# Sixteen K loads, one of them split into three DMAs: 64 partitions over 16 steps, and twice 32 partitions over 8 steps

## The chip, the cores and the metric

The kernel runs on one core of one Trainium2 chip. Its time is the device time of one execution in microseconds (us). An execution is also profiled; the profile's times are counted from the first instruction of the span.

## What is computed

One decode step (one new token, batch 8, width 512): attention over the last 2048 positions of a key/value cache with 32 query heads on 8 key/value heads, and then a small MLP block. For a sequence of one token the shifted branch of the MLP block is zero. Cut to what matters:

```python
W = 2048                                   # the last W of 8192 positions
q = layernorm(x) @ wq                      # (8, 32 heads, 128)
k, v = k_cache[:, :, Sk-W:, :], v_cache[:, :, Sk-W:, :]   # (8, 8, 2048, 128) bf16 each
p = softmax(q @ k^T * 128**-0.5)           # 4 query heads share one k and v
h = x + (p @ v) @ wo                       # wo (4096, 512)
x1 = layernorm(h)                          # the shifted branch adds 0
out = h + x1 + gelu(layernorm(x1) @ w3) @ w4
```

All inputs are bf16. The K and V windows are 33.5 MB each, 79 MB are read in all.

## The kernel before

The 64 pairs of batch and key/value head are called items, i = 8 * batch + head. One loop over steps `p` puts out the program for all engines; each engine works its instructions off in that order and waits on semaphores. At step p the loop emits:

- for p a multiple of 4, one K load (`load_k`, L337) for the four items p to p+3. There are 16 such loads, j = p // 4. Load j goes to buffer j % 3 of `knat` and has that buffer's semaphore;
- the 16 TensorE transposes of item p (`pe_T`, L244, recorded on L249), in two halves, and their copies from PSUM to `kT_sb` (`evict`, L256), one half by ScalarE (L257) and one by VectorE (L259);
- at p = 15, 23, 31 and 39 one of four loads of `wo`;
- the scores of item p - 2 (`pe_QK`, L263, recorded on L269) and, once a batch is complete, the steps of its softmax;
- the V load of item p - 13 (`load_v`, L343, 13 buffers) and its product with the probabilities (L327).

Loads of w3 and of w4 in three parts follow. All these loads but the small one of x are issued by SyncE, one after another in this order, on one queue (q1; recorded on L176). SyncE waits before a load until its buffer is free, and everything behind it waits too. The load of x (`x_sb`, 8 rows of 1 KB) is issued by ScalarE on its own queue (q10).

A K load moves 2 MB. A cache window of one item is 2048 rows of 128 elements. It is read as 32 runs of 64 rows, 16 KB each, and the run a of the item t goes to partition 4a + t, so that each of the 128 partitions gets one run:

```python
dma(SP, knat[:, j % NK, :],
    A_k_cache[i // G, i % G:i % G + KQ, W0:SK, :].rearrange("t (a c) d -> a t (c d)", c=KQ * NC),
    sem_k[j % NK], e_Thi.get(i + KQ - 1 - KQ * NK))
```

The last line is the load's semaphore and its wait: the transposes of the load that used the buffer before. A transpose of item i waits until `sem_k` of its buffer has 16 for every load into it so far (`K`, L236).

After the last item the tail runs: the last products, `wo`, the sums for the layernorm, `uT` (L460), the products with w3 (L475), the gelu (L500), the products with w4 (L513, which waits for the gelu and for the parts of w4) and the output.

Of the kernel before, what the change touches and what calls it, by code (L numbers as in the profile page):

```python
# [15 lines left out]
G = 8  # L16
R = H // G
SK = 8192
W = 2048
W0 = SK - W  # L20
NC = W // 128
# [5 lines left out]
NK = 3  # L27
KQ = 4
# [3 lines left out]
LV = 13  # L32
WO_AT = (15, 23, 31, 39)
NR = 4


class Engine:
# [29 lines left out]
def bass_sequential_preLN__sliding_block_cached__mixer_s_mlp__decode_kernel(  # L67
# [23 lines left out]
    with es:  # L91
# [28 lines left out]
        knat = sb([128, NK, KQ * NC * DH], dt.bfloat16, "knat")  # L120
# [46 lines left out]
        sem_k = [S(f"sem_k{i}") for i in range(NK)]  # L167
# [4 lines left out]
        PE, AC, DV, PO, SP = (Engine(S(n)) for n in ("s_pe", "s_act", "s_dve", "s_pool", "s_sp"))  # L172

        def dma(eng, dst, src, sem, *waits):
            def f(e):
                e.dma_start(dst, src).then_inc(sem, 16)  # L176
            eng.op(f, *waits, inc=False)
# [55 lines left out]
        e_Tlo, e_Thi, e_lo, e_hi, e_QK, e_PV = {}, {}, {}, {}, {}, {}  # L233
        e_max, e_mT, e_neg, e_negps, e_negc, e_exp, e_PT, e_pT, e_lsel, e_Lb, e_rL, e_scale = ({} for _ in range(12))

        def K(i):  # L236
            return sem_k[i // KQ % NK], 16 * (i // KQ // NK + 1)

        def V(i):
            return sem_v[i % NV], 16 * (i // NV + 1)  # L240
# [3 lines left out]
        def pe_T(i):  # L244
            def half(lo):
                def f(e):
                    for n in range(lo, lo + NC // 2):
                        r = NC * (n % KQ) + NC // KQ * (i % KQ) + n // KQ
                        ins = e.matmul(kT_ps[i % 2][:, n * 128:(n + 1) * 128],  # L249
                                       knat[:, i // KQ % NK, r * DH:(r + 1) * DH], ident_b[:, :], is_transpose=True)  # L250
                    return ins
                return f
            e_Tlo[i] = PE.op(half(0), K(i), e_lo.get(i - 2), e_idb)
            e_Thi[i] = PE.op(half(NC // 2), e_hi.get(i - 2))
# [79 lines left out]
                         e_rL[b], e_oz, *waits)  # L334


        def load_k(i):  # L337
            j = i // KQ
            dma(SP, knat[:, j % NK, :],
                A_k_cache[i // G, i % G:i % G + KQ, W0:SK, :].rearrange("t (a c) d -> a t (c d)", c=KQ * NC),  # L340
                sem_k[j % NK], e_Thi.get(i + KQ - 1 - KQ * NK))

        def load_v(i):  # L343
            dma(SP, vnat[:, i % NV, :].rearrange("p (c d) -> p c d", c=NC),
# [9 lines left out]
        def pe_wo_row(g):  # L354
            def f(e):
                for r in range(R):
                    h = R * g + r
                    ins = e.matmul(hrow[32 * r:32 * (r + 1), :], oT_all[:, h, :], wo_v[:, h, :],  # L358
                                   start=(g == 0), stop=(g == NR - 1),
                                   tile_position=(0, 32 * r), skip_group_check=True)  # L360
                return ins
            e = PE.op(f, e_sc7[g], e_scale[NB - 2], (sem_wo, 16 * len(WO_AT)))
            if g == NR - 1:

                e = AC.op(lambda e: e.activation(hr[:, 0, :], hrow, ACT.Copy), e)  # L365
                e_wo.append(DV.op(lambda e: e.tensor_tensor(hr[:, 1, :], hrow, hr[:, 0, :], ALU.subtract), e))


        def pe_h0():
            def f(e):  # L370
                for nb in range(KC):
                    e.matmul(hT_ps[:, nb * B:(nb + 1) * B], x_sb[:, nb * 128:(nb + 1) * 128],
                             ident_b[0:B, 0:B], start=(nb == 0), stop=False, skip_group_check=True)
                for part in range(2):
                    for nb in range(KC):
                        ins = e.matmul(hT_ps[:, nb * B:(nb + 1) * B], hr[:, part, nb * 128:(nb + 1) * 128], selb[:, :],
                                       start=False, stop=False, skip_group_check=True)
                return ins
            PE.op(f, e_wo[-1], e_exp[NB - 2], X, e_selb)

        def pe_wo(g):
            def f(e):
                for h in range(R * g, R * (g + 1)):
                    for nb in range(KC):
                        ins = e.matmul(hT_ps[:, nb * B:(nb + 1) * B], wo_v[:, h, nb * 128:(nb + 1) * 128],
                                       oT_all[:, h, 0:B], start=False, stop=(h == H - 1), skip_group_check=True)
                return ins
            e_wo.append(PE.op(f, e_sc7[g]))
# [3 lines left out]
        for p in range(NITEM + LV + 1):  # L392
            if p < NITEM:
                if p % KQ == 0:
                    load_k(p)
                pe_T(p)
                evict(p)
            if p in WO_AT:
                n = WO_AT.index(p)
# [18 lines left out]
            i = p - LV  # L418
            if 0 <= i < NITEM:
# [7 lines left out]
                else:  # L427
                    dst = kbank[g % 3][:, 0:R]
# [3 lines left out]
            g = i - 1 - G * LAST  # L432
            if g == NR:
                pe_h0()
            if 0 <= g < NR:
                pe_wo_row(g)
            elif g >= NR:
                pe_wo(g)
# [5 lines left out]
        for n in range(3):  # L444
            lo, hi = W4_AT[n:n + 2]
# [117 lines left out]
```

## Time and profile before

| | |
|---|---|
| Time, median of 3 runs (lowest to highest) | 200.28 us (200.23 to 200.66) |
| Time of the profiled execution | 200.67 us |
| Its span in the profile | 198.6 us |
| TensorE busy | 158.0 us (80%) |
| ScalarE busy | 84.7 us (43%) |
| VectorE busy | 70.6 us (36%) |
| Moved by DMA | 79.56 MB, 401 GB/s over the span |
| K loads: 16 of 2048 KB, median from issue to landing | 19.1 us |
| V loads: 64 of 512 KB, median from issue to landing | 19.6 us |
| Mean granted TensorE clock | 0.882 |

A busy engine is not yet the one that bounds the time: the chain of waits, followed back from the last instruction, tells what the end hung on. A DMA's time to landing runs from its issue to its completion and contains the time that it stands in the queue behind other loads. The DMA share is the mean over the core's 16 DMA engines, so a share of half can be eight engines at work and eight idle. A load is cut into packets, one for each contiguous run, and each engine that takes part ends with one small completion packet.

### The profile page before, as it was taken

How to read it: one execution, taken by the hardware profiler on the slowest of the kernel's cores; microseconds unless marked ns; L12 is line 12 of the kernel's file. 1: busy time of each engine (PE TensorE's matmuls, PEld its weight loads, DVE VectorE, ACT ScalarE, POOL GpSimd, SP SyncE). 2: the span in 40 equal slices, each digit the busy share in tenths (PEclk: the TensorE clock that was granted, in tenths of full speed). 3: DMA queues.
4: the chain of work that ended last, by engine and by line, in shares of the span. 5: the costliest groups of instructions: out<-in, count | busy, mean ns of one | idle time of the engine just before them, and what ended most of it. 6: DMA issues, size and time to landing. Idle time of an engine off the chain costs nothing.

```text
span 198.6 us, 5886 instructions
## 1 busy us (share of the span) xinstructions
PE 158.0 (80%) x2725; PEld 117.5 (59%) x2725; DVE 70.6 (36%) x167; ACT 84.7 (43%) x92; POOL 3.5 (2%) x11
## 2 busy tenths in 40 slices
PE   0037999889999299947999199969997999969853
PEld 0037766567766277635776076747774767556753
DVE  6101545533543033511444024422542344233240
ACT  6001666864574037522465045544554464420330
POOL 7000000000000000000000000000000000000000
PEclk9999999999999669995799969996999699965555
DMA  6999999999999999999999999999999999999970
GB/s 233 449 412 429 426 422 398 422 407 434 412 396 436 406 452 392 414 422 420 429 394 437 406 439 409 449 398 450 395 443 405 443 403 416 419 417 416 404 244 23
DMA packets 18280, 79.56 MB, mean 401 GB/s; under 512 B 1480, under 2 KB 7376, under 8 KB 16080
## 3 DMA queue, kind: packets, MB, share of 16 engines
q1 hardware_dynamic: 18240, 79.18, 97.3%
q8 instruction: 21, 0.34, 0.6%
q14 instruction: 3, 0.02, 0.0%
q10 hardware_dynamic: 16, 0.01, 0.0%
HBM read 79.18 MB, written 0.01 MB: 399 GB/s over the span
## 4 chain that ended last, share of the span: by engine, by line
DMA 66%; PE 28%; SPq 4%; issue 0%; DVE 0%
DMA knat<-in_A_k_cache_dram 56%; PE kT_ps L249 16%; DMA w_sb<-in_B_w_dram 10%; PE S_ps L269 6%; SPq L176 4%; PE oT_ps L327 3%; PE S_ps L513 1%; PE sm L305 0%; PE sm L282 0%; PE sm L317 0%; PE sm L291 0%; PE sm L521 0%; DVE fT L518 0%; DVE out_sb L522 0%
## 5 line engine op out<-in xcount | busy, mean ns | idle before, releaser
L257 ACT ACTIVATE kT_sb<-kT_ps 128x1024 bf16<-128x1024 bf16 x64 | 65.6, 1024 | 89.8 <-PE kT_ps L249 89.8
L249 PE MATMUL kT_ps<-ident_b,knat 128*128 128x128 bf16 x1024 | 76.0, 234 | 18.3 <-DMA knat<-in_A_k_cache_dram 18.3
L249 PEld LDWEIGHTS kT_ps<-ident_b,knat 128*128 128x128 bf16 x1024 | 65.5, 106 | 24.2 <-DMA knat<-in_A_k_cache_dram 19.2
L259 DVE COPY kT_sb<-kT_ps 128x1024 bf16<-128x1024 bf16 x64 | 44.3, 692 | 93.2 <-PE kT_ps L249 93.2
L327 PEld LDWEIGHTS oT_ps<-pT_sb,vnat 128*128 128x128 bf16 x896 | 26.5, 97 | 24.6 <-issue 22.3
L269 PE MATMUL S_ps<-kT_sb,qblk 128*32 128x512 bf16 x256 | 41.1, 611 | 0.0
L327 PE MATMUL oT_ps<-pT_sb,vnat 128*128 128x4 bf16 x896 | 31.3, 165 | 0.0
L295 ACT ACTIVATE P_sb<-S_ps,negcol 128x512 bf16<-128x512 f32 x8 | 11.2, 1401 | 5.9 <-DVE negcol L294 5.9
L269 PEld LDWEIGHTS S_ps<-kT_sb,qblk 128*32 128x32 bf16 x256 | 7.2, 94 | 5.4 <-issue 1.4
L219 PE MATMUL S_ps<-xlnT,wbig 128*128 128x8 bf16 x128 | 3.6, 168 | 7.7 <-DMA wbig<-in_A_wq_dram 7.7
L219 PEld LDWEIGHTS S_ps<-xlnT,wbig 128*128 128x128 bf16 x128 | 3.5, 104 | 7.8 <-issue 7.8
L278 DVE TENSOR_REDUCE mcol<-S_ps 128x1 f32<-128x512 f32 x8 | 5.5, 682 | 1.9 <-PE S_ps L269 1.9
L305 PE MATMUL sm<-ident_b,P_sb 128*128 128x128 bf16 x32 | 3.3, 231 | 2.7 <-ACT P_sb L295 2.7
L327 PEld LDWEIGHTS kT_ps<-pT_sb,vnat 128*128 128x128 bf16 x128 | 4.2, 106 | 1.8 <-issue 1.3
L226 DVE TENSOR_SCALAR qblk<-S_ps 128x32 bf16<-128x32 f32 x8 | 0.9, 182 | 11.1 <-PE S_ps L219 11.1
L309 DVE COPY pT_sb<-sm 128x512 bf16<-128x512 bf16 x8 | 3.3, 417 | 3.4 <-PE sm L305 3.4
L327 PE MATMUL kT_ps<-pT_sb,vnat 128*128 128x4 bf16 x128 | 4.5, 167 | 0.0
L207 PE MATMUL sm<-ident_b,xln_b 8*128 8x8 bf16 x4 | 0.3, 175 | 5.2 <-DVE xln_b L198 5.2
L305 PEld LDWEIGHTS sm<-ident_b,P_sb 128*128 128x128 bf16 x32 | 2.1, 102 | 3.2 <-ACT P_sb L295 3.2
L365 ACT ACTIVATE hr<-kT_ps 128x512 bf16<-128x512 f32 x1 | 0.6, 597 | 6.6 <-PE kT_ps L358 6.6
L317 PE MATMUL sm<-lsel,ones_f 128*128 128x32 f32 x16 | 3.2, 281 | 0.3 <-DVE lsel L313 0.3
L291 PE MATMUL sm<-ones_f,negrow 1*128 1x1 f32 x16 | 3.2, 266 | 0.1
(75 smaller groups left out, 63.2 us busy)
## 6 DMA issues: line engine op xcount, KB each, us to landing
knat<-in_A_k_cache_dram SPq DMA_DIRECT2D x16, 2048.0 KB, 19.1
vnat<-in_A_v_cache_dram SPq DMA_DIRECT2D x64, 512.0 KB, 19.6
wbig<-in_A_wq_dram SPq DMA_DIRECT2D x1, 4096.0 KB, 12.3
wbig<-in_A_wo_dram SPq DMA_DIRECT2D x4, 1024.0 KB, 21.6
w_sb<-in_B_w_dram SPq DMA_DIRECT2D x1, 1792.0 KB, 17.9
w_sb<-in_B_w_dram SPq DMA_DIRECT2D x1, 1280.0 KB, 20.1
w_sb<-in_B_w_dram SPq DMA_DIRECT2D x1, 384.0 KB, 17.5
w_sb<-in_B_w_dram SPq DMA_DIRECT2D x1, 128.0 KB, 7.6
```

The costliest lines, as they stand in the source:

```text
L176: e.dma_start(dst, src).then_inc(sem, 16)
L219: ins = e.matmul(S_ps[0][:, h * B:(h + 1) * B], wq_v[:, kc, h * DH:(h + 1) * DH], xlnT[:, kc * B:(kc + 1) * B], start=(kc == 0), stop=(kc ...
L249: ins = e.matmul(kT_ps[i % 2][:, n * 128:(n + 1) * 128], knat[:, i // KQ % NK, r * DH:(r + 1) * DH], ident_b[:, :], is_transpose=True)
L257: e_lo[i] = AC.op(lambda e: e.activation(kT_sb[:, i % NKT, 0:W // 2], kT_ps[i % 2][:, 0:W // 2], ACT.Copy), e_Tlo[i], e_QK.get(i - NKT))
L259: e_hi[i] = DV.op(lambda e: e.tensor_copy(kT_sb[:, i % NKT, W // 2:W], kT_ps[i % 2][:, W // 2:W]), e_Thi[i], e_QK.get(i - NKT))
L269: ins = e.matmul(S_ps[b % 2][32 * u:32 * (u + 1), :], qblk[:, b, g - g % KQ + t, :], kT_sb[:, i % NKT, :].rearrange("p (n t) -> p t n", t= ...
L278: e_max[b] = DV.op(lambda e: e.tensor_reduce(mcol[:, :], S_ps[b % 2][:, :], AX.X, ALU.max), e_QK[G * b + G - 1], e_mT.get(b - 1))
L291: e_negps[b] = PE.op(lambda e: e.matmul(sm[:, NEG], negrow[0:1, :], ones_f[0:1, 0:1], start=True, stop=True), e_neg[b], e_ones)
L295: e_exp[b] = AC.op(lambda e: e.activation(P_sb[:, j, :].rearrange("p (c a w) -> p c w a", c=4, w=KQ), S_ps[j][:, :].rearrange("p (c w a) - ...
L305: ins = e.matmul(pT_ps[:, jt * 128:(jt + 1) * 128], P_sb[:, j, 128 * jt:128 * (jt + 1)], ident_b[:, :], is_transpose=True)
L309: e_pT[b] = DV.op(lambda e: e.tensor_copy(pT_sb[:, j, :, :].rearrange("p (q jt) h -> p q jt h", jt=4), pT_ps[:, 0:NC * H].rearrange("p (jt ...
L327: ins = e.matmul(dst, vnat[:, i % NV, c * DH:(c + 1) * DH], pT_sb[:, b % 2, (c + NC // KQ * (i % KQ)) % NC, R * g:R * (g + 1)], start=(c = ...
```

## The change

The load j = 8 (items 32 to 35, the K of batch 4's first four heads) is issued as three DMAs. The first takes the runs 0 to 15 and writes partitions 0 to 63; the second and the third take 8 runs each and write partitions 64 to 95 and 96 to 127. The same bytes go to the same places. The three share the buffer's semaphore, so the load adds 48 to it in place of 16, and the transposes that wait for this buffer (j = 8, 11 and 14) wait for 32 more. All other loads stay as they are, and the instructions of TensorE, VectorE, ScalarE and GpSimd keep their order.

```diff
+K8 = 8
...
         def K(i):
-            return sem_k[i // KQ % NK], 16 * (i // KQ // NK + 1)
+            j = i // KQ
+            return sem_k[j % NK], 16 * (j // NK + 1 + (2 if j >= K8 and j % NK == K8 % NK else 0))
...
         def load_k(i):
             j = i // KQ
-            dma(SP, knat[:, j % NK, :],
-                A_k_cache[i // G, i % G:i % G + KQ, W0:SK, :].rearrange("t (a c) d -> a t (c d)", c=KQ * NC),
-                sem_k[j % NK], e_Thi.get(i + KQ - 1 - KQ * NK))
+            src = A_k_cache[i // G, i % G:i % G + KQ, W0:SK, :].rearrange("t (a c) d -> a t (c d)", c=KQ * NC)
+            dst = knat[:, j % NK, :]
+            if j == K8:
+                for lo, n in ((0, 16), (16, 8), (24, 8)):
+                    dma(SP, dst[KQ * lo:KQ * (lo + n), :], src[lo:lo + n], sem_k[j % NK],
+                        e_Thi.get(i + KQ - 1 - KQ * NK))
+            else:
+                dma(SP, dst, src, sem_k[j % NK], e_Thi.get(i + KQ - 1 - KQ * NK))
```

## The prediction

> **What bounds the kernel now.** I read the page's chain and DMA queues first, then the chain in order of time near the end, the DMA's busy share by slices over the last 10 us, and SyncE's timeline around the changed load.
>
> ```profile
> DMA 66%; PE 28%; SPq 4%; issue 0%; DVE 0%
> q1 hardware_dynamic: 18240, 79.18, 97.3%
> q8 instruction: 21, 0.34, 0.6%
> q10 hardware_dynamic: 16, 0.01, 0.0%
> ```
>
> The chain is two thirds DMA, and q1, SyncE's queue, keeps the 16 engines at work for 97.3% of the span. The kernel is a stream of loads that hardly pauses. A load has landed when the slowest engine has done its share, so the slowest engine sets the pace.
>
> ```profile
> 142.68 21.14 DMA knat<-in_A_k_cache_dram
> 163.82 0.05 issue
> 163.87 1.07 PE kT_ps L249 x16
> ...
> 174.12 20.07 DMA w_sb<-in_B_w_dram
> 194.19 0.14 issue
> 194.33 1.65 PE S_ps L513 x56
> ```
>
> In the chain (start, length, what) the last K load lands at 163.82 and the big w4 part at 194.19. TensorE had idled only 0.47 us before 163.87: it follows the K landings closely. From there the compute path reaches the end of the last gelu (L500) at 193.75 + 0.39 = 194.14. Loads and compute arrive at L513 together.
>
> ```profile
> DMA  9999999999999999998655555554622222110000
> ```
>
> This is the DMA share from 186 to 196 us in slices of 0.25 us. It falls to half and stays there from 191.0 to 192.75, then to a fifth and to nothing. Half of the engines have nothing left while the other half works on for 2 us and more. The packet records of the trace say who they are. Packets of one engine follow each other at exact distances (16 KB 0.607 us, 4 KB 0.155 us), so the 16 sequences can be told apart. Eight of them also carry q8's 21 code fetches of 16 KB in turn, and each fetch holds its engine up by 1.42 us. Call these the heavy engines and the others the light ones. The heavy ones end each load later:
> - V18, the load just before the changed one: light mean 83.63, heavy mean 85.10, lag 1.47 us
> - the changed load, K8: light up to 89.10, heavy up to 90.70
> - the last K load: light up to 160.81, heavy up to 163.82
> - the last V load: light up to 182.03, heavy up to 186.08
>
> **The change part by part.** *Packets.* Before, K8 gave each engine 8 packets of 16 KB. The first part has 64 packets over 16 steps, four for each of 16 engines. The other two have 8 steps of 4 each. How a load of 8 steps spreads is shown by q10: x_sb has 8 rows, and its 16 packets are 8 of data and 8 completions, so eight engines. (q1's sum confirms the counting: 144 for wq, 80 x 144 for K and V, 4 x 1040 for wo, 528 + 1840 for w3 and w4, and 48 for the output make 18240, with 16 completions each.) So the two small parts go to eight engines, four packets each time. These eight now have 12 packets, the rest 4: +4 x 0.607 = +2.43 us and -2.43 us.
>
> *Which eight.* Three of x_sb's engines can be followed by their exact distances, and as far as the sequences can be told apart all three are light ones. I take it that the eight are the light engines. The Trainium skill ("DMA: Bandwidth & Descriptors", on why a DMA increments its semaphore by 16) says it is the lowest-numbered ones on this path; the trace has no engine numbers, so no row confirms that.
>
> *Best case, every engine at its own rate.* Light engines end K8 at 89.10 + 2.43 = 91.53 instead of 90.70 overall (+0.8). The last K lands at max(160.81 + 2.44, 163.82 - 2.43) = 163.25 (-0.57), the last V at 184.47 (-1.6), and w3 and w4 behind it likewise.
>
> *Worst case, two engines that write the same partitions halve each other.* Every load but the small x_sb spreads over 128 partitions, and the packet distances stay rigid however far the engines drift apart. That is what one sees if every engine has its own eight partitions and meets nobody there. The change is the first to break this: partitions 0 to 63 are written by all 16 engines, then 64 to 127 by eight, while the heavy engines, which must own half of the 128, write them too. Pair a light engine with the heavy one whose partitions it enters, lag d. In the first part the light one is alone for d and shares the remaining 2.43 - d, which takes twice as long. While the heavy one does the rest of its four packets, the light one is alone in the upper half for d; its remaining 4.86 - d is shared with V packets, twice as long again. The light engine needs d + 2(2.43 - d) + d + 2(4.86 - d) = 14.58 - 2d instead of 4.86, and the heavy one loses the shared time and saves 2.43. With d = 1.47 that is +6.8 and +1.9 us. Light engines then set the pace: the last K at 160.81 + 6.8 = 167.6 (+3.8), the last V at 182.03 + 6.8 = 188.8 (+2.7), w3 and w4 behind it (+2.7).
>
> No row shows two engines on one stripe for long, so the bounds stand at none and full. I take the full price, because the rigid distances are the nearest row: 16 engines that collided at random would show stretched K and V packets without a fetch beside them. The Trainium skill speaks against the change too ("SBUF — State Buffer", Door 1): 0 to 63 reach 8 of 16 write ports and were measured at 196 GB/s for 1 MiB. No run here shows that; as an estimate from it, two such halves take 10.7 us instead of 4.9 and the time would be about 206.
>
> *Issue.*
>
> ```profile
> 78.19 0.82 SPq L176 DMA_DIRECT2D knat<-in_A_k_cache_dram  x1
> ...
> 84.44 17.67 SPq L176 DMA_DIRECT2D vnat<-in_A_v_cache_dram  x1
> ```
>
> Two more DMA instructions cost about 0.55 us each (the K issues of 0.55) on SyncE. Four V loads and K9 (81.12) are queued behind them. I cost this at nothing: what is issued at 79 lands at 92, and SyncE then sits 17.67 us in one V issue with its queue full. Without this cover it would be 1.1 us. The wait at L249 now needs all three parts, and behind it stand the transposes of items 32 to 35, the scores and the PV of V19 on. It is the landing above and adds nothing more. Work on TensorE, ScalarE and VectorE is unchanged.
>
> *Sum.* With the last K 3.8 us late, compute from 163.87 on moves by 3.8. One wait goes: L475 began at 190.64, just after w3 landed (190.54, by its issue at 172.64 + 17.9), while uT was done at 190.08 + 0.19 = 190.27. Now uT comes at 194.07, w3 at 193.2, so 0.27 us is won back. The gelu ends at 194.14 + 3.8 - 0.27 = 197.67; w4 landed at 194.19 + 2.7 = 196.9 and no longer matters. L513 starts 0.19 after the gelu at 197.86 instead of 194.33: +3.5 us. The rest, 4.3 us to the end, is the same. The profiled execution took 200.67 us (span 198.6 and 2.07 around it) and would take 204.2; against the median of 200.28 it is 203.8. Lags from 1.0 to 2.0 us give +7.7 to +5.7 instead of +6.8, so +2.4 to +4.4. A pair with almost no lag (84.31 against 84.24) would give light +9.6, the last K at 170.4 and about 206.6. Own range 202.3 to 206.5.
>
> **The rivals.** *Balance: each engine keeps its rate (faster).* Late engines hand 64 KB each to early ones. For it: the half-empty slices at the end, and that light and heavy differ by 3 to 4 us. Against it: the argument of rigid distances. The last K lands 0.57 us earlier, of which TensorE's idle 0.47 can be won; the wait for w3 (0.27) goes; w4 lands at 192.6, before the gelu. L513 starts at 194.14 - 0.47 - 0.27 + 0.19 = 193.59, 0.74 earlier: 199.5 us. It decides if halves can be written at full rate, that is if K8 lands before about 92.
>
> *The small parts fall on the heavy engines.* Against it: x_sb's three. Without sharing the last V lands 2.43 late and the time is 202.7; with sharing the lag counts the other way, the late ones get later by over 9 us, and it is about 208.
>
> *The change does not do what it says: 8 steps still spread over 16 engines.* Then q1 has 18272 packets, bytes per engine stay, and the time is 200.3, or up to 4.9 more if each part is held to half the partitions' rate. Against it: x_sb's eight completions.
>
> **How the numbers follow.** Full or nearly full sharing on light engines 0.58; balance 0.24; heavy engines 0.10 (two thirds of it beyond my range); 16 engines 0.08, half of it with no change. A measurement of this kernel can tell about 0.2% from no change, 0.4 us. Faster 0.24; same 0.04; slower 0.58 + 0.10 + 0.04 = 0.72. The time is that of the likeliest, 203.8. The range takes in the balance case with 0.5 us below it, 199.0, and reaches up to 206.5; what is left out is about 0.15.
>
> **What would show it.** In the profile after: 18256 packets on q1 (18240 - 144 + 80 + 40 + 40) for eight engines. K8's transposes starting after 94 rather than at 91.5. GB/s in the slices of 88 to 98 us well below the 392 to 452 elsewhere, since engines wait for each other while half of the partitions are idle. The last K landing near 167.6, L513 waiting for ScalarE rather than for w_sb. I am wrong if GB/s stays above 400 there and K8 lands by 92: then nothing is shared and the end comes earlier; or if the half-busy shelf at the end grows longer, which would mean that the heavy engines took the parts.

## The result and the profile after

The changed kernel takes 209.71 us (median of 4 runs, 209.43 to 210.68) against 200.27 us (200.23 to 200.66): a ratio of 1.0475, 95% interval 1.0439 to 1.0512. The profiled execution took 209.43 us with a span of 207.4, which is 8.76 and 8.8 us more than before. The direction was forecast; the size was not, and the time lies 3.2 us above the range.

The page of the changed kernel: the line of the shares, the queue, and the GB/s of 40 slices of 5.2 us each.

```profile
DMA 46%; PE 42%; SPq 4%; ACT 4%; DVE 2%; issue 1%; ACTq 0%
...
q1 hardware_dynamic: 18256, 79.18, 97.0%
...
GB/s 261 449 395 423 433 420 384 448 397 443 395 427 404 445 403 402 270 217 217 366 404 393 430 420 427 419 423 426 416 435 413 431 415 412 418 417 417 389 230 11
```

18256 packets confirm the count: the two parts of 8 steps went to eight engines each. The queue works for 97.0% of the span as before, so the engines do not stand still. But from slice 17 to slice 20 they move 217 to 270 GB/s and then 366 in place of some 420. (The page's DMA digit is 9 in each of these slices.)

The same in stretches of 5 us, changed kernel first, then the kernel before. The columns are the stretch, its length, busy time and instructions of each engine, granted TensorE clock, DMA share, GB/s.

```profile
85.00:90.00 5.00, 1.55 (x29) 0.85 (x25) 0.69 (x1) 1.02 (x1) 0.00 (x0) 1.00 0.97 212
90.00:95.00 5.00, 0.00 (x0) 0.00 (x0) 0.00 (x0) 0.00 (x0) 0.00 (x0) 0.57 1.01 212
95.00:100.00 5.00, 0.00 (x0) 0.00 (x0) 0.00 (x0) 0.00 (x0) 0.00 (x0) 0.50 1.00 221
100.00:105.00 5.00, 4.41 (x56) 3.58 (x56) 0.76 (x2) 1.55 (x2) 0.00 (x0) 0.57 1.00 414
```

```profile
85.00:90.00 5.00, 1.91 (x36) 1.26 (x33) 0.69 (x1) 1.02 (x1) 0.00 (x0) 1.00 0.98 414
90.00:95.00 5.00, 4.21 (x50) 3.58 (x51) 0.69 (x1) 1.36 (x2) 0.00 (x0) 0.54 1.06 437
95.00:100.00 5.00, 5.00 (x80) 3.60 (x77) 2.38 (x5) 2.13 (x3) 0.00 (x0) 0.78 0.98 411
```

For 15 us the DMA share stays at 1 while the rate is half, and TensorE has nothing to do from 90 to 100. At 100 both are as they were. The packet records show the same more sharply: of the packets of 4 and 16 KB that start between 84 and 100 us not one has its usual duration. The 4 KB ones take mostly 0.28 to 0.33 us instead of 0.159, the 16 KB ones 1.1 to 1.3 instead of 0.611 (and less only where they run on past 100). This holds for the V packets of all 16 engines too, and not only for those that meet an engine of K8.

The chain of the changed kernel in order of time:

```profile
79.38 21.16 DMA knat<-in_A_k_cache_dram
...
149.50 23.79 DMA knat<-in_A_k_cache_dram
173.34 1.07 PE kT_ps L251 x16
...
199.63 0.59 PE kT_ps L483 x16
...
201.47 1.28 ACT L508
...
203.06 1.67 PE S_ps L521 x56
```

(All lines lie 2 to 8 further down: L251, L483, L508 and L521 are L249, L475, L500 and L513 of before.) K8 lands at 100.55 (before 90.70). The last K lands at 173.30 (before 163.82, +9.48), and L521 starts at 203.06 (before 194.33, +8.73). w4 no longer stands ahead of L521: the gelu does. The compute path made up 0.75 us, of which some 0.3 is the wait for w3 that the forecast saw go (from the end of uT to the first product with w3 it is 0.06 us, before 0.37); the rest is spread over the steps after 173.34.

At the end of the loads, 195 to 205 us of the changed kernel in slices of 0.25 us:

```profile
DMA  9999899999999999887754325111111110000000
```

The half-busy shelf did not grow, it is gone; two engines alone work for the last 2 us. Followed by their packet distances, these two are heavy engines that had taken small parts.

### The profile page after: what moved, and what is told of

Same layout as the page of the kernel before. It is cut to its first block, busy times and chain, and to the rows that moved or that the text cites. A ratio compares the mean times of both kernels' runs of the same rounds, so it can differ in the third digit from the quotient of the medians.

```text
span 207.4 us, 5888 instructions
## 1 busy us (share of the span) xinstructions
PE 158.0 (76%) x2725; PEld 117.2 (56%) x2725; DVE 70.6 (34%) x167; ACT 84.4 (41%) x92; POOL 3.5 (2%) x11
## 3 DMA queue, kind: packets, MB, share of 16 engines
q1 hardware_dynamic: 18256, 79.18, 97.0%
## 4 chain that ended last, share of the span: by engine, by line
DMA 46%; PE 42%; SPq 4%; ACT 4%; DVE 2%; issue 1%; ACTq 0%
DMA knat<-in_A_k_cache_dram 46%; PE kT_ps L251 19%; PE S_ps L271 9%; PE oT_ps L329 6%; SPq L177 4%; PE kT_ps L329 2%; ACT P_sb L297 1%; PE kT_ps L366 1%; PE S_ps L393 1%; PE S_ps L521 1%; PE sm L307 1%; PE sm L284 1%; PE sm L293 1%; ACT L508 1%; ACT L297 1%
## 5 line engine op out<-in xcount | busy, mean ns | idle before, releaser
L251 PE MATMUL kT_ps<-ident_b,knat 128*128 128x128 bf16 x1024 | 75.7, 234 | 26.8 <-DMA knat<-in_A_k_cache_dram 26.8
L251 PEld LDWEIGHTS kT_ps<-ident_b,knat 128*128 128x128 bf16 x1024 | 65.3, 105 | 32.4 <-DMA knat<-in_A_k_cache_dram 27.4
L271 PE MATMUL S_ps<-kT_sb,qblk 128*32 128x512 bf16 x256 | 41.1, 612 | 0.0
L284 PE MATMUL sm<-ident_f,mcol 128*1 128x128 f32 x16 | 3.0, 271 | 0.3 <-DVE mcol L280 0.3
```

What stands on the lines that cost most here:

```text
L251: ins = e.matmul(kT_ps[i % 2][:, n * 128:(n + 1) * 128], knat[:, i // KQ % NK, r * DH:(r + 1) * DH], ident_b[:, :], is_transpose=True)
L271: ins = e.matmul(S_ps[b % 2][32 * u:32 * (u + 1), :], qblk[:, b, g - g % KQ + t, :], kT_sb[:, i % NKT, :].rearrange("p (n t) -> p t n", t= ...
L284: e_mT[b] = PE.op(lambda e: e.matmul(sm[0:1, MROW], mcol[:, :], ident_f[:, :], start=True, stop=True), e_max[b], e_rL.get(b - 1), e_idf)
```

## The experiments

Three theories stood after the result. *Destination*: engines that write the same partitions at the same time share a fixed rate. *Imbalance*: nothing is shared, and the price is that eight engines do 12 packets of K8 and eight do 4. *Count*: more DMAs, completions or smaller pieces cost by themselves. The kernel before was run beside each group: 200.61, 200.59 and 200.68 us. Only K8 differs in each kernel. The diffs show its loop, against the changed kernel (where only + lines stand, they take the place of that loop); the number of semaphore steps follows the number of DMAs.

**Two halves over all 16 engines.**

```diff
-                for lo, n in ((0, 16), (16, 8), (24, 8)):
+                for lo, n in ((0, 16), (16, 16)):
```

> K8 in two DMAs of 64 partitions, 16 steps each: all 16 engines keep 8 packets of K8, q1 has 18256 packets (18240 + 16). Destination theory (engines that meet in one half of the partitions share its rate): each half of 1 MB moves at half of 430 GB/s, so K8 takes about 9.7 us instead of 4.86, nothing is won back, and the time is 200.3 + 4.9 = about 205. Imbalance theory (the cost comes from eight engines having 192 KB and eight 64 KB): bytes per engine are as before, 200.3. Count theory (more and smaller DMAs cost): two DMAs instead of three, half of the change's 9.4, also about 205; the column split tells it from the first.

Measured 205.79 us, ratio 1.024 (1.017 to 1.0311). No engine has more packets of K8 than another and the kernel is still 5 us slower, so imbalance alone falls as the cause. The chain and a long stretch of this kernel:

```profile
84.00:95.00 11.00, 2.82 (x56) 1.86 (x52) 1.18 (x2) 1.40 (x2) 0.00 (x0) 0.74 1.00 228
```

```profile
147.26 21.84 DMA knat<-in_A_k_cache_dram
169.10 0.05 issue
```

The rate is halved from 84 to 94.9. Half of 10.9 us is 5.4, and the last K lands 5.3 later than before.

**Small parts first, then a half.**

```diff
-                for lo, n in ((0, 16), (16, 8), (24, 8)):
+                for lo, n in ((0, 8), (8, 8), (16, 16)):
```

> The change with its parts the other way round: two of 32 partitions and 8 steps for partitions 0 to 63, then one of 64 partitions and 16 steps for 64 to 127. Bytes per engine and per group as in the change. Destination theory, if the eight engines' own partitions are 0 to 63: they write the small parts at full rate beside the others, and only the last part is shared, so about 4.9 us less halving than in the change: 203 to 206. Destination theory, if their own are 64 to 127: the small parts meet the others' packets, as costly as the change or more, 209 to 211. Imbalance theory: like the change, 209.7.

Measured 205.62 us, ratio 1.0224 (1.0166 to 1.0283). Eight engines have 12 packets here as in the changed kernel, and yet it takes 4 us less.

```profile
83.00:88.00 5.00, 4.16 (x83) 2.97 (x79) 1.41 (x3) 2.05 (x2) 0.00 (x0) 1.00 1.04 431
88.00:95.00 7.00, 0.00 (x0) 0.00 (x0) 0.00 (x0) 0.00 (x0) 0.00 (x0) 0.65 1.04 238
96.00:100.00 4.00, 3.29 (x41) 2.65 (x42) 0.69 (x1) 1.02 (x1) 0.00 (x0) 0.50 1.02 424
```

While the eight write partitions 0 to 63 the rate is full; it halves only when all 16 write 64 to 127 (by the packets 88.2 to 95.9). So partitions 0 to 63 are the usual ones of the eight that take parts of 8 steps. In the changed kernel their small parts went to 64 to 127, the usual ones of the other eight. That a DMA has few steps or uses few engines is not what halves the rate: the same two small parts run at full rate when they go to 0 to 63.

**Three DMAs by columns**, each over all 128 partitions.

```diff
-                for lo, n in ((0, 16), (16, 8), (24, 8)):
-                    dma(SP, dst[KQ * lo:KQ * (lo + n), :], src[lo:lo + n], sem_k[j % NK],
+                for lo, hi in ((0, 4096), (4096, 6144), (6144, 8192)):
+                    dma(SP, dst[:, lo:hi], src[:, :, lo:hi], sem_k[j % NK],
```

> K8 in three DMAs that each write all 128 partitions, one half and two quarters of the columns (8, 4 and 4 KB packets), 16 engines each: the same number and the same sizes of DMAs as in the change. Destination theory: no engine leaves its own partitions, 200.3 (within 0.3). Imbalance theory: 200.3. Count theory: the whole 9.4, about 209.7.

Measured 200.67 us, ratio 1.0001 (0.9964 to 1.0037), with 18528 packets and no dip, so count falls as the cause:

```profile
85.00:90.00 5.00, 1.86 (x35) 1.22 (x32) 0.69 (x1) 1.02 (x1) 0.00 (x0) 0.99 1.01 415
```

**An 8-step view of a full-width half.**

```diff
+                dma(SP, dst[:, 0:4096], src[:, :, 0:4096], sem_k[j % NK], e_Thi.get(i + KQ - 1 - KQ * NK))
+                dma(SP, dst[:, 4096:8192], src[:, :, 4096:8192].rearrange("(a e) t n -> a e t n", a=8), sem_k[j % NK],
+                    e_Thi.get(i + KQ - 1 - KQ * NK))
```

> K8 in two DMAs that each write all 128 partitions: half of the columns as before, the other half with a source of 8 steps. If the 8 steps hold, eight engines have 192 KB and eight 64 KB of K8, as in the change (q1 18248 packets: 18240 + 128 + 8 - 128 with 8 completions for the second), but the eight write into all 128 partitions. Imbalance theory: like the change, 209.7. Destination theory: only half of the 128 KB that each of the eight writes in the second part goes into partitions of others, so at most half of the change's cost, 202 to 205. If the steps are merged to 32, 16 engines share it evenly (18384 packets) and the time is 200.3.

Measured 200.52 us, ratio 0.9982 (0.9953 to 1.001). q1 has 18384 packets, which is 16 completions for each of two DMAs: the view of 8 steps went to 16 engines like one of 32. The run therefore says nothing on eight engines; it is one more split by columns that costs nothing.

**The place read or the place written?** Partitions and runs had gone together so far: who writes 0 to 63 reads the first half of each window. Two kernels part them. Both leave the positions of these four items in another order in the buffer.

```diff
+                for m in range(2):
+                    half = A_k_cache[i // G, i % G:i % G + KQ, W0 + 1024 * m:W0 + 1024 * (m + 1), :]
+                    dma(SP, dst[:, 4096 * m:4096 * (m + 1)], half.rearrange("t (a c) d -> a t (c d)", c=KQ * NC // 2),
+                        sem_k[j % NK], e_Thi.get(i + KQ - 1 - KQ * NK))
```

> Load 8 as two DMAs that each read one half of the four items' windows (positions 0 to 1023, then 1024 to 2047) as 32 runs of 8 KB, and write all 128 partitions, one half of the columns each. The positions of these four items lie in another order in the buffer than the reference has them, nothing else changes. Each DMA reads just the bytes that a half-partition DMA read, but from no engine's view leaves its own partitions. If the place that is written is what halves the rate, nothing is halved: 8 KB packets near 0.31 us, slices of 84 to 96 us near 400 GB/s, the last K near 163.8, time 199.9 to 201.3. If the place that is read is what halves it (only half of the window read at a time), the slices fall to about 220 GB/s for some 10 us and the time is 205 to 206.5, as with two half-partition DMAs of 16 steps.

```diff
+                for m in range(2):
+                    dma(SP, dst[64 * m:64 * (m + 1), :], src[m:32:2], sem_k[j % NK],
+                        e_Thi.get(i + KQ - 1 - KQ * NK))
```

> Load 8 as two DMAs of 16 steps over 64 partitions each, as in the kernel with two halves, but each reads every second run of the window (the even ones, then the odd ones), so that both read over the whole window. The positions of these four items lie in another order in the buffer than the reference has them, nothing else changes. If the place that is written is what halves the rate: as with two halves, GB/s near 220 for about 10 us, last K near 169, time 205 to 206.5. If the place that is read is what halves it: no dip, last K near 163.8, time 199.9 to 201.3.

The stretch of 84 to 94 us, first of the kernel that halves what is read, then of the one that halves what is written:

```profile
84.00:94.00 10.00, 5.78 (x86) 4.49 (x83) 1.38 (x2) 2.05 (x2) 0.00 (x0) 0.72 1.03 427
```

```profile
84.00:94.00 10.00, 2.22 (x45) 1.51 (x41) 0.69 (x1) 1.02 (x1) 0.00 (x0) 0.74 1.01 222
```

The first takes 200.84 us, ratio 1.0003 (0.9975 to 1.0031), its 8 KB packets 0.309 us. The second takes 205.97, ratio 1.0262 (1.0235 to 1.0289). Which partitions are written decides. Which half of the window is read does not.

**Who are the eight?** K8 only as its first 16 runs, in two parts of 8 steps; the other runs are left out.

```diff
-                for lo, n in ((0, 16), (16, 8), (24, 8)):
+                for lo, n in ((0, 8), (8, 8)):
```

> Load 8 issues only its runs 0 to 15, as two DMAs of 8 steps (partitions 0 to 31 and 32 to 63); the runs 16 to 31 are left out, so partitions 64 to 127 of the buffer keep older data. If the small parts go to eight engines, these keep their usual 8 packets of 16 KB and the other eight have none (-8 x 0.607 = -4.86 us for them). If those eight own partitions 0 to 63 nobody meets anybody, and the slices of 84 to 96 us stay near 400 GB/s. This tells who the eight are. Eight light engines (what the forecast took): their ends stay (last K 160.8, last V 182.0), the heavy ones come 4.86 earlier, so the last K lands near 160.8 and the last V near 182. Six light and two heavy engines: the two heavy ones keep their ends, the last K lands near 163, the last V near 184.2, and the time is 198.5 to 200.2. If the eight do not own 0 to 63, the slices fall to about 220 GB/s and the last K lands later than 163.8.

```profile
140.36 22.75 DMA knat<-in_A_k_cache_dram
163.11 0.05 issue
```

The last K lands at 163.11, not at 160.8, although the other eight engines have nothing to do for K8. The rate stays full (426 GB/s from 85 to 90). So some of the eight are heavy: by the packet sequences six light ones and two heavy ones, which end the last K at 162.8 and 163.04 in the kernel before. The time is 200.21 us, ratio 0.9979 (0.9951 to 1.0007), at the upper edge of what was expected (198.5 to 200.2) and not distinct from before: what the last K gains is small, and the profiled execution (199.32) was the shortest of ten.

**Who is slowed down?** The same kernel with two more DMAs of one run for each item: 4 packets of 16 KB to partitions 64 to 67, and 4 to 96 to 99. The other 14 runs of the upper half are left out.

```diff
-                for lo, n in ((0, 16), (16, 8), (24, 8)):
+                for lo, n in ((0, 8), (8, 8), (16, 1), (24, 1)):
```

> As the kernel that loads only runs 0 to 15 of load 8 in two 8-step parts, plus two single runs of four partitions (64 to 67 and 96 to 99); the other runs of load 8 are left out. Each single run is 4 packets of 16 KB on four engines, so at most four to eight engines write into partitions of others. If a meeting slows only the engines that meet there, only the packets of those engines and of the one or two owners are stretched: GB/s falls by a fifth or a third for 2 to 5 us, most 4 KB packets keep 159 ns beside some of 300 ns and more, and the time stays within 1.5 us of that kernel. If any meeting slows the whole DMA system, all 4 KB packets go to about 300 ns while it lasts, GB/s falls to about 220, and the last K lands 2 us or more later than there. If four packets at a time into one engine's place are held to that one place's rate, packets of 16 KB take 2.4 us and more (four times 0.61).

Measured 203.38 us (the profiled execution took 204.79, the longest of five), ratio 1.0109 (1.0061 to 1.0157), 3.2 us more than without the two small DMAs. The stretch of 89 to 92 us, first of this kernel, then of the one without:

```profile
89.00:92.00 3.00, 0.00 (x0) 0.00 (x0) 0.00 (x0) 0.00 (x0) 0.00 (x0) 0.58 1.02 104
```

```profile
89.00:92.00 3.00, 1.97 (x20) 1.73 (x20) 0.04 (x1) 0.90 (x1) 0.00 (x0) 0.50 1.03 431
```

128 KB bring all 16 engines down to a quarter. 18192 packets on q1 (16 more) say that four engines carry each of these DMAs. Their 16 KB packets take 2.52 us, four times 0.61 and more: four engines together bring into this place 26 GB/s (64 KB in 2.52 us), about what one engine brings alone (16 KB in 0.607 us, 27 GB/s). And no packet of 4 KB that starts between 89 and 92 us takes less than 0.629 us, four times its usual 0.159; the V packets of the twelve engines without a run are among them. A meeting does not slow down only those who meet. It slows down everybody, as much as those who meet. Why, no run here shows. Here the expectation of a local effect falls, and the size under "whole system" (half) was too small as well: four at one place give a quarter.

**The change at load 3.**

```diff
-K8 = 8
+K8 = 3
```

> The change at load 3 (items 12 to 15) in place of load 8, where the engines have drifted apart less. If the lag between engines gave relief (14.58 - 2d), less lag means a higher price: the last K lands 1 to 3 us later than in the changed kernel (173.3), the time 210.5 to 212.5. If the lag gives none, because all 16 engines are halved as long as any engine writes into the foreign half, the price is the same: last K 172.5 to 174, time 208.5 to 210.5, with GB/s near 220 for about 16 us from load 3's first packets on. If the price came from what stands behind load 8 only (the chain hangs on the late K landings), an early delay could be made good before the end, and the time would be below 206; the queue never empties, so I do not expect that.

```profile
GB/s 273 423 408 423 433 275 216 204 400 395 398 421 400 421 407 426 407 397 408 446 399 408 427 423 414 428 421 427 420 420 421 434 411 416 420 414 417 398 235 8
```

```profile
151.16 21.90 DMA knat<-in_A_k_cache_dram
173.10 1.07 PE kT_ps L251 x16
```

Measured 209.51 us, ratio 1.0426 (1.0381 to 1.047), and the last K lands within 0.3 us of the changed kernel's, 130 us after the disturbance. Less lag does not make the price higher, and nothing of the K loads' delay is made good on the way. By the packets the slow stretch lasts from 26.7 to 41.1, 14.4 us, against 16 at load 8. Lag does not shorten the stretch, if anything it lengthens it.

**One rule that fits all.** Take it that while n engines of the split load write into one place, every engine goes at 1/n. This was seen for two values only: a half where 16 engines write one half of the partitions, or eight write the usual ones of the other eight; a quarter where four engines write four partitions (there the engine whose usual partitions these are is not counted in n). Which partitions make up one place is not shown. By this rule the last K lands where the engine that ends it stood before, plus the time lost, plus 2.43 us (4 x 0.607) where that engine has four more packets. Starting points from the kernel before: 162.95, between their two ends, for the two heavy engines among the eight, and 163.82 for the latest of the others.

| Kernel | slow stretch by the packets, us | lost | sum for the last K | measured |
|---|---|---|---|---|
| the change | 84.0 to 99.9, half | 8.0 | 162.95 + 2.43 + 8.0 = 173.4 | 173.30 |
| the change at load 3 | 26.7 to 41.1, half | 7.2 | 162.95 + 2.43 + 7.2 = 172.6 | 173.06 |
| two halves | 84.0 to 94.9, half | 5.4 | 163.82 + 5.4 = 169.2 | 169.10 |
| small parts first | 88.2 to 95.9, half | 3.85 | 162.95 + 2.43 + 3.85 = 169.2 | 169.39 |
| lower runs only | none | 0 | 162.95 | 163.11 |
| with two single runs | 88.6 to 93.2, a quarter | 3.45 | 166.4, or 167.6 if that engine carries them (2 x 0.607) | 167.51 |

The stretches are read from the same runs, so the table shows that loss and landing go together; it does not predict the length of a stretch. That follows for the changed kernel from 12 packets of 1.22 us, 14.6, and the 1.47 us by which the engines start apart.

## Why the prediction was wrong

**What held.** Eight steps went to eight engines, and 18256 packets were counted. Engines that write the same partitions share a rate, which was the case taken as likeliest against balance. GB/s fell in 88 to 98, K8's transposes began after 94 (at 100.59), L513 came to wait for ScalarE, w3's wait of 0.27 went. From the last K's landing to the time the sum was right to half a us: 9.48 us later there, less 0.27, would be 9.2; the time of the profiled execution rose by 8.76.

**The term 14.58 - 2d failed.** The prediction paired each light engine with one heavy engine and gave the light one two stretches of the length d alone at full rate. The runs show that no engine goes on at full rate while others meet: the two halves over 16 engines put every engine at half from 84 to 94.9, and two single runs on four engines put all 16 at a quarter. So an engine still at its V packets is slowed by the others' early start, and one that has gone ahead by the others' late finish. With d = 1.47 this took 2.94 us off the sum; the changed kernel's slow stretch is even longer than 14.6. The argument of rigid distances was sound for whether a meeting costs, but its reading as a matter between two engines came from no row.

**"I take it that the eight are the light engines" failed.** Three of x_sb's engines were followed and light; eight were inferred. Two are heavy and end the last K near 162.95, not at 160.81: 2.14 us. Both errors are in the same direction: 167.6 + 2.94 + 2.14 = 172.7, against 173.30 measured; the 0.6 left is about the slow stretch's excess of 16 over 14.6, at half. The rival that gave the small parts to the heavy engines was thus a quarter true, and a quarter is enough, since a load lands with its slowest engine.

**The range.** Its upper end came from a pair with almost no lag on a light engine (206.6). No case inside it combined full sharing with a late engine; the rival that did was left outside. That rival's "about 208" was itself low by its own words: over 9 us on the late engines, carried on as in the forecast's sum, makes about 209.

**The issue's price was mis-sized, but covered.** SyncE's timeline of the changed kernel:

```profile
77.66 2.42 SPq L177 DMA_DIRECT2D knat<-in_A_k_cache_dram  x3
80.11 1.87 SPq L177 DMA_DIRECT2D vnat<-in_A_v_cache_dram  x4
```

Three issues took 2.42 us where one had taken 0.82, +1.6 instead of +1.1. The load by columns issues three DMAs as well and shows no loss.

**The rule of the Trainium skill.** "SBUF — State Buffer", Door 1, gives 196 GB/s for partitions 0 to 63 at 1 MiB; here the stretches of 5 and 10 us in which only one half is written by K8 show 212 to 222 GB/s for the whole queue, 8 to 13% more. The same table gives 27.6 GB/s for partitions 0 to 3; four packets of 16 KB in 2.52 us are 26 GB/s. The second agrees with the page, and the first is near it. The estimate from it (10.7 us for two halves, about 206) is close to what two halves over 16 engines took, 10.9 us and 205.79; the change went beyond it because its upper half took eight engines with eight packets each.

## What to carry to other kernels

Where a kernel lives on a full DMA queue as this one does, let every load write all 128 partitions; if one must be cut, cut it by columns, which cost nothing here in three ways of doing it. Judge a narrow load by what it does to every transfer in flight and not by its bytes: here one split load of 16 cost 4.75%, and two loads of 64 KB cost 3 us. Narrow alone is not dear: two loads of 32 partitions each, written by the engines that usually write there, went at full rate. And before a cost is laid on "the early engines", all of them have to be identified, since the latest one among them sets the landing.

## What was not expected of the hardware

- Transfers that meet nobody are slowed down by the meeting of others, at once and by the same factor: 4 KB packets went from 0.159 us to about 0.31 while 16 engines wrote one half of the partitions, and to 0.63 and more while four engines wrote four partitions. It ends when the meeting ends. Which resource passes the delay on to all 16 engines stays open; the runs show only that, for halves, it hangs on which partitions are written and not on which half of the window is read.
- A loss in the load stream was kept to the end: at load 3 it cost as much as at load 8 (209.51 and 209.71 us).
- A split source view was not taken by its outer count: 8 steps of 4 that follow each other were spread like 32 steps, over 16 engines.
